# Moving three W1 pieces, their sums and four tile statistics around the first block products of a spectral and Mish network

## Chip, core and metric

The kernel runs on one core of one Trainium2 chip. Its time is device microseconds (us). The time before is the median of eight runs; a profile of one further look at the same program gives the rows quoted here. Matmuls run on TensorE (PE in the profile, its weight loads PEld), elementwise work on VectorE (DVE), ScalarE (ACT) and GpSimd (POOL). SyncE (SP) issues most of the transfers, in the order of its own queue.

## What is computed

Four layers over x of 2048 tokens by 1024 features, two kinds in turn (A, B, A, B), each added to x after a layer norm:

```
x = x + A(norm(x))     # A: rfft2, multiply by w_r + i*w_i, irfft2
x = x + B(norm(x))     # B: h = x @ w1 + b1;  act = h * tanh(softplus(h));  act @ w2
x = x + A(norm(x))
x = x + B(norm(x))
```

w1 is 1024 x 3584 and w2 is 3584 x 1024, all in bf16. The change is in layer B, which runs twice with the same weights.

## The kernel before

Every engine has its own instruction list, written out by the program in order. A helper records what each buffer was last written and read by, and puts the needed semaphore waits in front of an instruction. An engine never passes a waiting instruction, so the order in which a list is written is the order of the work.

Layer B treats the tokens as 16 tiles of 128 (index j), in four chunks of 512 (index c). The features of w1 are cut into 14 pieces of 256 columns (index fg). Normalising a tile takes these steps on VectorE: `stats_dve` (L487: two bn_stats of 512 and one aggregation), `scales` (L491: eight operations on a few numbers for a reciprocal root), and `apply` (L514, its operation on L521), which writes the normalised tile. For the first two chunks the tile is transposed on TensorE. From tile 8 on, `turned` (L1120) puts eight transposing transfers of 128 x 128 into a list, and `turn(n)` (L1131) moves n of them into SP's queue.

The chunks 0 and 1 are first multiplied plainly with pieces 0 to 5 (`mm1`, L1135). Pieces 6 to 13 are then multiplied with both chunks at once by `quads` (L1180). It sees a piece and the two chunks as 2 x 2 blocks and forms the result from seven products of four matmuls instead of eight. For that it needs sums of blocks:

- of the tokens, made by `token_sums` (L1157) on VectorE: T1, T2 and T4 by the call with `last=False`, T3 by the second call (all on L1164);
- of the weights, S1 to S4, made by `fill_slot` (L1074) on GpSimd: after the load of the piece, four operations of 128 x 512 (L1084), and a store of the piece with its sums to `w1s_scratch` (L1086). In later uses of the piece, the second layer B among them, `fill_slot` loads the stored form and GpSimd has nothing to do.

All seven products of a piece wait for all of its sums (`product`, L1184, reads `s.res` and `s.rs`). With n counting the pieces of one call of `quads`, TensorE's order in round n is A11, S2 of this piece, then A22, S4 of the one before, then S1, A12, S3 of this piece. VectorE adds the partial results (`add`, L1192, its operation on L1193). The last product of a round, S3 with T3, adds onto the bank of the second product, S2 with T2, which VectorE must first have read with its add. So the S3 of the first round waits for T3 and for that add. `after(n-1)` (L1386) is called in the middle of round n, behind S4, and puts other work there: refills of slots, loads of w2, normalisations and transposing transfers.

A slot holds one piece with its sums, 7 KB in every partition. Three slots, `early`, take pieces 6, 7 and 8. Three more, `ws`, lie where the pieces 0 to 4 of `mm1` lay, so each can be filled when `mm1` of chunk 1 is through with the pieces under it: the first after piece 1, the second after piece 3, the third after piece 4. Pieces 9, 10 and 11 go there, pieces 12 and 13 follow in the first two of them as they come free.

In the version before, the early fills name the tile buffer `xn[7].res` as something that GpSimd reads (L1356), which is how its first sums are held back behind the `apply` of tile 7. The buffer's memory is used again by the second of the token sums. Behind `mm1` come, in this order: statistics of tiles 8 to 11 and their scales, `apply` of tile 8 and its eight transposes, the fills of pieces 9 to 11, and T3 (L1373 to L1384).

Of the kernel before, what the change touches and what calls it, by code (L numbers as in the profile page):

```python
# [180 lines left out]
class KB:  # L181
# [869 lines left out]
        self.dma(self.sp, dst, self.w1.rearrange("(db dp) f -> dp db f", dp=P)[:, :, fg * 256:(fg + 1) * 256], f"w1_{writes[0].name}",  # L1051
                 reads=after, writes=writes)

    def open_slots(self, name, off, n):

        slots = []
        for i in range(n):
            b = self.alloc(f"{name}{i}", off + 7168 * i, [3584])
            b.raw = b.ap[:, 0:2048].rearrange("p (d f) -> p d f", f=256)
            b.rs = Res(f"{name}s{i}")  # L1060
            b.rs.inherit(b.res)
            slots.append(b)
        return slots
# [24 lines left out]
    def layer_B(self, li, last):  # L1088
        pe, dve, act, sp, pool = self.pe, self.dve, self.act, self.sp, self.pool
# [5 lines left out]
        def open_xt(c):  # L1095
            off = self.ob[f"XT{c}"]
            XT[c] = self.alloc(f"XT{c}", off, [8, 512])
            r_xt[c] = self.sub_res(XT[c], f"xt{c}h", 2, off, 8192)
            for r in r_xt[c]:
                r.begin()  # L1100
# [19 lines left out]
        def turned(c, t, xn):  # L1120

            x, r = XT[c], r_xt[c][t // 2]
            for db in range(8):
                def one(db=db):
                    self.dma(sp, x.ap[:, db, t * P:(t + 1) * P], xn.ap[:, db * P:(db + 1) * P], f"xt{c}_{t}", reads=[xn.res],
                             parts=[r], transpose=True)
                    if db == 7:
                        xn.unread = False
                turning.append(one)

        def turn(n):  # L1131
            for _ in range(min(n, len(turning))):
                turning.pop(0)()

        def mm1(c, fg, half=None, mid=()):  # L1135
            wb = self.w1_buf[fg]
            x = XT[c]
            tok = slice(0, 512) if half is None else slice(256 * half, 256 * half + 256)
            w = tok.stop - tok.start
            for fl in range(2):  # L1140
                if fl:
                    for f in mid:
                        f()
                ft = 2 * fg + fl
                bank = nh[0] % 3
                nh[0] += 1
                fns = []
                for db in range(8):
                    fns.append(lambda e, db=db, bank=bank, fl=fl: e.matmul(  # L1149
                        PS[:, bank, 0:w], wb.ap[:, db, fl * P:(fl + 1) * P], x.ap[:, db, tok], start=(db == 0), stop=(db == 7)))  # L1150
                self.group(fns, reads=[wb.res] + (r_xt[c] if half is None else [r_xt[c][half]]), writes=[self.r_bank[bank]])
                at, ra = AT[c % 2], r_at[c % 2][ft]
                self.op(act, lambda e, bank=bank, ft=ft: e.activation(at.ap[:, ft, tok], PS[:, bank, 0:w], ACT.Mish,  # L1153
                                                                      bias=self.B1[:, ft:ft + 1]),
                        reads=[self.r_bank[bank], self.r_b1], writes=[ra])

        def token_sums(p, last=True):  # L1157

            c0, c1 = 2 * p, 2 * p + 1
            lo, hi = [[XT[c].ap[:, 4 * k:4 * k + 4, :] for c in (c0, c1)] for k in range(2)]  # L1160
            t3 = lo[1].bitcast(F16)
            both = r_xt[c0] + r_xt[c1]
            tt = lambda dst, x, y, reads, writes: self.op(
                dve, lambda e: e.tensor_tensor(dst, x, y, ALU.subtract), reads=reads, writes=writes)  # L1164
            if last:
                tt(t3, hi[1], lo[1], r_xt[c0], r_xt[c1])
                T = self.T
                return {"B11": (lo[0], r_xt[c0]), "B21": (hi[0], r_xt[c0]), "B22": (hi[1], r_xt[c1]), "T3": (t3, r_xt[c1]),
                        "T1": (T[0].ap, [T[0].res]), "T2": (T[1].ap, [T[1].res]), "T4": (T[2].ap, [T[2].res])}
            self.T = T = [self.alloc(f"TS{i}", self.ob["TS"] + 4096 * i, [4, 512], F16) for i in range(3)]  # L1170
            tt(T[0].ap, lo[1], lo[0], both, [T[0].res])
            tt(T[1].ap, hi[1], T[0].ap, both + [T[0].res], [T[1].res])
            tt(T[2].ap, hi[0], T[1].ap, both + [T[1].res], [T[2].res])
# [6 lines left out]
        def quads(fgs, slot_of, B, after=lambda n: None):  # L1180
# [25 lines left out]
            for n in range(N + 1):  # L1206
                if n < N:
                    a, b, d, p1, u2, u3, ft = parts(n)
                    product(n, a, "A11", "B11", True)
                    self.copy(act, p1.ap, PS[:, a, :], [self.r_bank[a]], [p1.res])  # L1210
                    product(n, b, "S2", "T2", True)
                    add(u2, b, p1)
                if n:
                    _, pb, pd, q1, q2, q3, pft = parts(n - 1)
                    mish(1, pft + 1, q3.ap, q3.res)
                    product(n - 1, pb, "A22", "T4", False)
                    add(q1, pb, q1)
                    mish(0, pft + 1, q1.ap, q1.res)
                    product(n - 1, pd, "S4", "B22", False)
                    add(q2, pd, q2)  # L1220
                    mish(1, pft, q2.ap, q2.res)
                    after(n - 1)
                if n < N:
                    product(n, d, "S1", "T1", True)
                    product(n, a, "A12", "B21", False)
                    mish(0, ft, PS[:, a, :], self.r_bank[a])
                    product(n, b, "S3", "T3", False)
                    add(u3, b, p1)
                    add(u3, d, u3)
# [37 lines left out]
        W2 = [[None] * 7, [None] * 7]  # L1267

        def load_w2(h, i):
            off = (28, 32, 120, 124, 92, 96, 100)[i] * 1024 if h else self.ob["W2"] + i * 4096  # L1270
            if h and not i and W2[1][0]:
                off = 104 * 1024
            W2[h][i] = self.alloc(f"W2_{h}_{i}", off, [4, 512])
            self.dma(sp, W2[h][i].ap, w2v[:, 4 * i:4 * i + 4, h * 512:(h + 1) * 512], f"w2_{h}_{i}", writes=[W2[h][i].res])
# [6 lines left out]
        xn = {}  # L1281
# [15 lines left out]
        def residual(j):  # L1297
            self.op(dve, lambda e: e.tensor_tensor(self.XS[:, j, :], self.XS[:, j, :], YS.ap[:, j - 4, :], ALU.add),
                    reads=[YS.res], writes=[self.r_xs[j]])
# [51 lines left out]
        self.scales(6, 2)  # L1351
        for j in (6, 7):
            xn[j] = self.apply(j)
        early = self.open_slots("WE", self.ob["W2"], 3)
        for n in range(3):
            self.fill_slot(early[n], 6 + n, [xn[7].res])  # L1356
        for fg in range(2):
            mm1(1, fg, 0, mid=turns(1, 2, 3) if fg else ())
        for fg in range(2):
# [1 line left out]
        def normal(j):  # L1361
            if j % 4 == 0:
                open_xt(j // 4)
            turned(j // 4, j % 4, self.apply(j))

        for fg in range(2, 6):
            mm1(1, fg)
            if fg < 4:
                for j in range(4 * fg, 4 * fg + 4):
                    residual(j)  # L1370
            if fg == 3:
                token_sums(0, last=False)
            if fg == 4:  # L1373
                for j in range(8, 12):
                    self.stats_dve(j)
        self.xn_buf = self.xn_out + [self.alloc(f"XN{i}", self.ob["XN2"] + i * 2048, [self.D]) for i in range(2)]
        self.scales(8, 4)
        normal(8)
        turn(8)
        ws = self.open_slots("WS", self.ob["WS"], 3)  # L1380
        for n in range(3):
            self.fill_slot(ws[n], 9 + n)
        order = early + [ws[n % 3] for n in range(5)]
        B = token_sums(0)  # L1384

        def after(n):  # L1386
            if n in (3, 4):
                self.fill_slot(order[n + 3], 9 + n)
            if 2 <= n < 6:
                for i in range(2 * n - 4, min(2 * n - 2, 7)):  # L1390
                    load_w2(0, i)
            if n < 3:
                normal(9 + n)
            elif n < 7:
                self.stats_dve(9 + n)
            turn(4)
        quads(list(range(6, 14)), order, B, after)
        for i in range(7):
# [1 line left out]
        order = [ws[(n + 2) % 3] for n in range(14)]  # L1400
# [2 lines left out]
        self.xn_buf = [self.alloc(f"XN{i}", self.ob["TS"] + i * 2048, [self.D]) for i in range(4)]  # L1403
        for n in range(16):
            if n == 0:
                self.scales(12, 4)
            if n < 4:
                normal(12 + n)
            t = n % 8
            mm2(t // 4, t % 4, n // 8)  # L1410
            turn(4)
            if n == 10:
                token_sums(1, last=False)
                B = token_sums(1)
# [64 lines left out]
```

## Time and profile before

| | |
|---|---|
| median of 8 runs | 1005.75 us (1002.58 to 1008.11) |
| the profiled execution | 1005.08 us, its span 1003.3 us |
| TensorE busy | 923.3 us, 92% of the span, mean granted clock 0.983 |
| VectorE, ScalarE, GpSimd busy | 509.9, 377.4 and 157.5 us |
| first layer B: block products of pieces 6 to 13 | 173.64 to 244.84 us |
| second layer B: the same | 671.34 to 720.84 us |

All times in the rows are us from the start of the span, unless marked ns. A timeline row has its start, its length, engine, source line, operation, output and inputs, a count, and in brackets how long the engine had stood idle and what released it. A row with a count above one is a merged stretch. A row of the table by stretches has, for each engine, its busy time and its number of instructions, then the granted TensorE clock as a share of full speed.

### The profile page before, as it was taken

The page shows a single profiled execution, that of the slowest core. Times are in us where ns is not written, and L with a number is a line of the kernel's source. Part 1 is how long each engine was busy: PE and PEld are TensorE (multiplying, and loading weights), DVE is VectorE, ACT ScalarE, POOL GpSimd, SP SyncE. Part 2 cuts the span into 40 slices and gives each one's busy share as a digit, 9 for nine tenths or more (in the row PEclk, how much of TensorE's full clock was granted, in tenths as well). Part 3 has the DMA queues.
Part 4 walks back from the last instruction along what each step waited for, and adds up shares of the span by engine and source line. Part 5 has one row for each costly group of instructions (what it writes and reads, how often), then busy time and mean ns, then how long its engine had stood idle before and what let it go on. Part 6 is the DMA issues. An engine that isn't in the chain of part 4 may idle for free. (4 is left out here: it accounts for less than half of the span.)

```text
span 1003.3 us, 13599 instructions
## 1 busy us (share of the span) xinstructions
PE 923.3 (92%) x5572; PEld 489.4 (49%) x5650; DVE 509.9 (51%) x931; ACT 377.4 (38%) x531; POOL 157.5 (16%) x184
## 2 busy tenths in 40 slices
PE   0799699688999999999998997999999999999998
PEld 0667475233444444444446765754444444444443
DVE  6797468755327555524335864686611325551111
ACT  7898484243000155510007974745400015550000
POOL 4831007063500060000431200000000000000000
PEclk9999799889999999999999998999999999999999
DMA  9969732387721154230850797205761114421000
GB/s 285 278 198 323 199 98 88 88 242 226 239 61 48 43 210 152 106 110 26 206 117 20 219 227 189 111 6 179 252 215 29 45 44 162 158 95 63 32 32 21
DMA packets 140430, 136.47 MB, mean 136 GB/s; under 512 B 74368, under 2 KB 121296, under 8 KB 140368
## 3 DMA queue, kind: packets, MB, share of 16 engines
q1 hardware_dynamic: 127264, 95.26, 32.4%
q0 software_dynamic: 10928, 38.69, 11.9%
q10 hardware_dynamic: 2176, 1.66, 0.5%
q8 instruction: 44, 0.72, 0.3%
q14 instruction: 18, 0.15, 0.0%
HBM read 97.49 MB, written 33.55 MB: 131 GB/s over the span
## 5 line engine op out<-in xcount | busy, mean ns | idle before, releaser
L1239 PE MATMUL PS<-ARENA 128*128 128x512 bf16 x1756 | 385.6, 380 | 1.9
L1188 PE MATMUL PS<-ARENA 128*128 128x512 f16 (+1 forms) x1210 | 273.5, 385 | 20.7 <-DVE ARENA L1193 11.9
L1239 PEld LDWEIGHTS PS<-ARENA 128*128 128x128 bf16 x1792 | 174.9, 98 | 212.0 <-DVE ARENA L1193 0.8
L1193 DVE TENSOR_TENSOR ARENA<-PS,ARENA 128x512 f32<-128x512 f32 x220 | 152.1, 691 | 113.2 <-PE PS L1188 111.6
L1188 PEld LDWEIGHTS PS<-ARENA 128*128 128x128 bf16 x1232 | 120.8, 99 | 172.7 <-DVE ARENA L1193 15.9
L1251 DVE TENSOR_TENSOR XS<-PS,XS 128x512 bf16<-128x512 f32 x63 | 43.6, 691 | 271.1 <-PE PS L1239 271.1
L577 ACT ACTIVATE ARENA<-PS 128x512 f32<-128x512 f32 (+2 forms) x66 | 51.8, 784 | 265.1 <-PE PS L1188 254.1
L1198 ACT ACTIVATE ARENA<-ARENA,B 128x512 bf16<-128x512 f32 x132 | 95.2, 721 | 64.2 <-DVE ARENA L1193 58.2
L1084 POOL TENSOR_TENSOR ARENA<-ARENA 128x512 bf16<-128x512 bf16 x56 | 67.5, 1205 | 130.9 <-DMA ARENA<-in_B_w_dram 67.4
L1149 PE MATMUL PS<-ARENA 128*128 128x256 bf16 (+1 forms) x570 | 86.7, 308 | 0.4
L1149 PEld LDWEIGHTS PS<-ARENA 128*128 128x128 bf16 x576 | 55.4, 98 | 26.6 <-DVE ARENA L1115 0.7
L469 DVE BATCH_NORM_STATS2 BN<-XS 128x6 f32<-128x512 bf16 x99 | 64.2, 677 | 5.8 <-DMA XS<-in_A_x_dram 4.8
L1153 ACT ACTIVATE ARENA<-PS,B 128x256 bf16<-128x256 f32 (+1 forms) x72 | 38.3, 541 | 35.5 <-PE PS L1149 35.0
L1198 ACT ACTIVATE ARENA<-PS,B 128x512 bf16<-128x512 f32 x44 | 30.2, 687 | 19.4 <-PE PS L1188 19.4
L441 ACT ACTIVATE RS<-MV,EPS 128x2 f32<-128x2 f32 (+2 forms) x5 | 1.5, 298 | 95.6 <-DVE MV L472 83.7
L802 PE MATMUL PS<-ARENA 128*128 128x256 bf16 x256 | 32.4, 273 | 3.9 <-DVE ARENA L791 3.2
L780 ACT ACTIVATE ARENA<-PS 128x1024 bf16<-128x1024 f32 x32 | 33.4, 1074 | 4.5 <-PE PS L776 4.5
L728 PE MATMUL PS<-FD,ARENA 128*128 128x256 bf16 (+1 forms) x256 | 31.8, 271 | 2.4 <-DVE ARENA L646 1.3
L1023 PE MATMUL PS<-MT,ARENA 128*128 128x32 bf16 (+1 forms) x512 | 21.9, 203 | 11.2 <-DMA ARENA<-u_scratch 7.8
L784 DVE TENSOR_TENSOR ARENA<-ARENA 128x1024 bf16<-128x1024 bf16 x32 | 22.0, 687 | 19.3 <-ACT ARENA L780 13.7
L813 ACT ACTIVATE ARENA<-PS 128x1024 bf16<-128x1024 f32 x28 | 30.0, 1094 | 3.8 <-PE PS L802 3.8
L802 PEld LDWEIGHTS PS<-ARENA 128*128 128x128 bf16 x256 | 24.0, 98 | 12.0 <-DVE ARENA L791 5.7
(95 smaller groups left out, 693.2 us busy)
## 6 DMA issues: line engine op xcount, KB each, us to landing
ARENA<-in_B_w_dram SPq DMA_DIRECT2D x62, 512.0 KB, 6.4
ARENA<-w1s_scratch SPq DMA_DIRECT2D x30, 896.0 KB, 4.6
w1s_scratch<-ARENA POOLq DMA_DIRECT2D x14, 896.0 KB, 4.1
u_scratch<-ARENA SPq DMA_DIRECT2D x14, 512.0 KB, 3.5
ARENA<-u_scratch SPq DMA_DIRECT2D x14, 512.0 KB, 6.1
w_scratch<-ARENA POOLq DMA_DIRECT2D x8, 512.0 KB, 7.2
ARENA<-w_scratch POOLq DMA_DIRECT2D x8, 512.0 KB, 5.6
out_dram<-XS SPq DMA_DIRECT2D x16, 256.0 KB, 2.0
```

Of the source, the lines that this page charges most:

```text
L469: self.op(self.dve, lambda e: e.bn_stats(self.BN[:, j, 6 * h:6 * h + 6], self.XS[:, j, 512 * h:512 * h + 512]), reads=[self.r_xs[j]], part ...
L577: fn = (lambda e: e.activation(dst, src, ACT.Copy)) if scale is None else \
L780: self.op(act, lambda e: e.activation(x.ap.rearrange("p a b -> p (a b)"), ps, ACT.Copy, scale=SIG), reads=banks, writes=[x.res])
L802: fns.append(lambda e, c=c, part=part: e.matmul(ps[:, c * 256:(c + 1) * 256], yk.ap[:, part, c * P:(c + 1) * P], t[:, (128, 0)[part]:(384, ...
L1084: self.op(self.pool, lambda e, dst=A(dst), x=A(x), y=A(y), op=op: e.tensor_tensor(dst, x, y, op), reads=[b.res] + list(after), writes=[b.rs])
L1149: fns.append(lambda e, db=db, bank=bank, fl=fl: e.matmul(PS[:, bank, 0:w], wb.ap[:, db, fl * P:(fl + 1) * P], x.ap[:, db, tok], start=(db ...
L1153: self.op(act, lambda e, bank=bank, ft=ft: e.activation(at.ap[:, ft, tok], PS[:, bank, 0:w], ACT.Mish, bias=self.B1[:, ft:ft + 1]), reads= ...
L1188: self.group([lambda e, db=db: e.matmul(PS[:, bank, :], A[:, db, :], mov[:, db, :], start=(start and db == 0), stop=(db == 3), skip_group_ ...
L1193: self.op(dve, lambda e: e.tensor_tensor(dst.ap, PS[:, bank, :], x.ap, ALU.add), reads=[self.r_bank[bank], x.res], writes=[dst.res])
L1198: self.op(act, lambda e: e.activation(at.ap[:, ft, :], src, ACT.Mish, bias=self.B1[:, ft:ft + 1]), reads=[res, self.r_b1], writes=[ra])
L1239: fns.append(lambda e, i=i, ft=ft, w=W2[h][ft // 4]: e.matmul(PS[:, bank, :], at.ap[:, ft, t * P:(t + 1) * P], w.ap[:, ft % 4, :], start=( ...
L1251: self.op(dve, lambda e: e.tensor_tensor(xs, PS[:, bank, :], xs, ALU.add), reads=[self.r_bank[bank]], writes=[self.r_xs[j]])
```

## The change

The early fills now wait for a resource `gate` that stands for VectorE's instruction count behind the `apply` of tile 7; they no longer name the buffer as read. Slots of `ws` are opened and filled one by one inside the loop of `mm1`: piece 9 before `mm1` of piece 2, piece 10 before that of piece 4, piece 11 before that of piece 5. In front of the block products stand only the statistics and scales of tiles 8 and 9, and four of the transposes of tile 8. Statistics of tiles 10 and 11 go behind products 1 and 2, their scales behind product 3, and their `apply` behind products 3 and 4. Statistics of tiles 12 and 13 go behind products 5 and 6, those of 14 and 15 behind the block products. The same is written for both layers B.

```diff
-    def open_slots(self, name, off, n):
+    def open_slots(self, name, off, *ids):
         slots = []
-        for i in range(n):
+        for i in ids:
...
-        early = self.open_slots("WE", self.ob["W2"], 3)
+        gate = Res("gate")
+        gate.set_w(dve, dve.count)
+        early = self.open_slots("WE", self.ob["W2"], 0, 1, 2)
         for n in range(3):
-            self.fill_slot(early[n], 6 + n, [xn[7].res])
+            self.fill_slot(early[n], 6 + n, [gate])
...
+        ws = []
         for fg in range(2, 6):
+            if fg in (2, 4, 5):
+                ws += self.open_slots("WS", self.ob["WS"], len(ws))
+                self.fill_slot(ws[-1], 8 + len(ws))
             mm1(1, fg)
...
             if fg == 4:
-                for j in range(8, 12):
+                for j in range(8, 10):
                     self.stats_dve(j)
+        order = early + [ws[n % 3] for n in range(5)]
+        self.scales(8, 2)
         self.xn_buf = self.xn_out + [self.alloc(f"XN{i}", self.ob["XN2"] + i * 2048, [self.D]) for i in range(2)]
-        self.scales(8, 4)
         normal(8)
-        turn(8)
-        ws = self.open_slots("WS", self.ob["WS"], 3)
-        for n in range(3):
-            self.fill_slot(ws[n], 9 + n)
-        order = early + [ws[n % 3] for n in range(5)]
+        turn(4)
         B = token_sums(0)
 
         def after(n):
...
-            if n < 3:
-                normal(9 + n)
-            elif n < 7:
-                self.stats_dve(9 + n)
+            if n in (1, 2, 5, 6):
+                self.stats_dve((0, 10, 11, 0, 0, 12, 13)[n])
+            if n == 3:
+                self.scales(10, 2)
+            if n in (0, 3, 4):
+                normal((9, 0, 0, 10, 11)[n])
             turn(4)
...
             if n == 0:
+                self.stats_dve(14)
+                self.stats_dve(15)
                 self.scales(12, 4)
```

## The prediction

> **What bounds the kernel now.** I first read the table by stretches for the two runs of the same work, the block products of pieces 6 to 13 in the first and in the second layer B (columns: busy time of PE, PEld, DVE, ACT, POOL; granted clock; DMA share; GB/s).
>
> ```profile
> 173.64:244.84 71.20, 54.94 (x222) 22.96 (x225) 45.04 (x78) 26.47 (x39) 26.45 (x26) 0.88 0.61 181
> 671.34:720.84 49.50, 48.49 (x222) 21.73 (x225) 35.13 (x55) 26.67 (x39) 0.00 (x0) 1.00 0.61 189
> ```
>
> The same matmuls take 71.2 us in the first layer and 49.5 in the second, where GpSimd does nothing. So the first layer has 21.7 us that can be won, and the second next to nothing. TensorE's own timeline shows where they are.
>
> ```profile
> 173.64 3.87 PE L1188 MATMUL PS<-ARENA 128*128 128x512 bf16 x16
> 185.52 14.68 PE L1188 MATMUL PS<-ARENA 128*128 128x512 f16 x59 [8.02 <-DVE ARENA L1193]
> 203.70 21.00 PE L1188 MATMUL PS<-ARENA 128*128 128x512 bf16 x82 [3.50 <-POOL ARENA L1084]
> 228.37 13.95 PE L1188 MATMUL PS<-ARENA 128*128 128x512 bf16 x55 [3.67 <-POOL ARENA L1084]
> 243.10 1.90 PE L1188 MATMUL PS<-ARENA 128*128 128x512 f16 x8 [0.79 <-DVE ARENA L1193]
> ```
>
> Three waits: 8.0 us before the S3 product of the first round, 3.5 us for the sums of piece 9, 3.7 us for those of piece 12. The 0.8 at the end stands in the second layer too. After each of the three, weight loads start 0.43 us apart instead of 0.213: for 3.3, 5.5 and 3.4 us, which costs half of that, 1.6, 2.7 and 1.7 us. Waits and half speed make 22 us, the excess. What ends the first wait is VectorE's list, what ends the others is GpSimd's and SP's:
>
> ```profile
> 168.94 2.17 DVE L1164 TENSOR_TENSOR ARENA<-ARENA 128x2048 f16<-128x2048 bf16 x1
> 173.46 2.48 DVE L1164 TENSOR_TENSOR ARENA<-ARENA 128x2048 f16<-128x2048 bf16 x2 [2.35 <-POOL ARENA L1084]
> ...
> 183.65 1.22 DVE L1164 TENSOR_TENSOR ARENA<-ARENA 128x2048 f16<-128x2048 bf16 x1
> 184.78 0.68 DVE L1193 TENSOR_TENSOR ARENA<-PS,ARENA 128x512 f32<-128x512 f32 x1
> ```
>
> ```profile
> 167.30 6.06 POOL L1084 TENSOR_TENSOR ARENA<-ARENA 128x512 bf16<-128x512 bf16 x4
> 173.65 0.56 POOL L251 DMA_DIRECT2D w1s_scratch<-ARENA  x1 [0.30 <-POOL ARENA L1084]
> 198.81 4.83 POOL L1084 TENSOR_TENSOR ARENA<-ARENA 128x512 bf16<-128x512 bf16 x4 [24.60 <-DMA ARENA<-in_B_w_dram]
> ```
>
> ```profile
> 183.76 10.66 SPq L250 DMA_TRANSPOSE ARENA<-FD  x8
> 194.46 2.39 SPq L251 DMA_DIRECT2D ARENA<-in_B_w_dram  x3
> ```
>
> VectorE: T1, a wait for GpSimd, T2 and T4, from 175.86 to 183.7 the statistics, scales and `apply`, then T3 and the add that frees TensorE. GpSimd: 24.6 us idle for the load of piece 9. SP: that load is queued behind eight transposes, which could not start before `apply` of tile 8.
>
> **The change part by part.** I call r the time at which TensorE resumes with the first round's S3; before, r = 185.5.
>
> *The gate.* T2 no longer waits 2.35 us for GpSimd. But it now runs beside GpSimd's last sums, as T1 did: 2.17 us against 1.22 alone. T1 ends at 171.1, T2 at about 173.3; T4 waits for the end of GpSimd's last sum, itself put off to about 174.2, and ends at 175.4 instead of 175.9. Gain 0.5 us (at most 2.35, at least 0).
>
> *Two statistics fewer.* Four tiles took 175.86 to 181.5, 1.4 us each. Two less: gain 2.8 us. bn_stats doesn't suffer from GpSimd: a pair takes 1.28 us at 234.32, inside a stretch of sums, and 1.28 at 175.86 outside one. They come back behind products 1 and 2, and 5, 6 and the last, where VectorE has room: in a round of 5.97 us five adds of 0.69 take 3.5, and the same 1.5 us stood behind products 3 to 6 before at no cost in the second layer. Without that cover each would cost 1.4.
>
> *GpSimd busy where it was idle.* The three loads no longer wait behind transposes but on `mm1`: they can go out at about 160, 167 and 170 and land 6 to 7 us later. GpSimd then goes from piece 8 straight to pieces 9, 10, 11, four sums at a pitch of 1.23 us and a store of 0.9 each: ready at about 180, 186 and 192. This puts sums beside VectorE's scales, `apply` and T3, which had GpSimd idle before. No row shows a small operation of the scales beside a sum. Bounds: below, no delay, since bn_stats and the adds from PSUM (0.69 at 209.04, beside sums) have none. Above, each of the ten operations waits out most of a sum. The Trainium skill, page "SBUF — State Buffer", section "Who interferes with whom", speaks for the upper end, and so against this change: an operation with two SBUF inputs, or in a two-port mode, contends with a GpSimd operation that reads SBUF, and the loser is blocked for the whole of it. Trace: T1 lost 0.95, the residual additions went at one per 1.56 us beside sums against 0.61 in a row alone (4.89 for eight), and `apply` at 210.67 took 1.03 instead of 0.55 while the sum behind it was put off by only 0.07. So a sum holds the port for some 0.9 of its 1.23 us and leaves 0.3 free. By the rule taken as one operation per sum: 8 scales x 1.23 = 9.9, `apply` 1.4, T3 2.2, add 0.7, from 178.2 (175.4 + 2.8): r = 192.4. By the row's free 0.3 us, in which one or two operations of 0.16 fit, and with GpSimd's 0.9 us for a store in between: scales 2.7 instead of 1.6, `apply` 1.4, T3 2.1, add 0.7: r = 185.1. Without any delay: 178.2 + 1.6 + 0.55 + 1.2 + 0.7 = 182.3. I take r = 185.2, nearest to the `apply` row. So the first wait shrinks by 0.3 us only; the 3.3 us of the two parts above go into the port.
>
> *The second wait.* TensorE comes to piece 9 15 products after r, 14.7 us, at about 199.9. The sums are there at 180. Gone: 3.5 us, and with it the half speed behind it, 2.7. The page "TensorE: Matmul & The Clock Gate" (its Part 1) says that the half rate follows an idle window of about 3.4 us on a free-running grid; a wait of 3.5 would rarely hold a whole one, so by the rule 2.7 of this stays. The row has half speed for 5.5 us behind just this wait: I count 6.2.
>
> *The third wait.* The slot of piece 12 comes free with the S4 of piece 9, 26 products after r, at r + 24.1 = 209.3. Before, the same point was 215.8, and the load went out at 216.86 since SP was still at four transposes of 6.55. After, SP has eight transposes less in front of the fills and four fewer in all by then; it is through at about 207. So 1.0 us is won here. Then as before 6.6 us to GpSimd's start and 4.9 for sums: TensorE goes on at 220.9, having arrived at 218.1. The wait stays, 2.8 us.
>
> *What is late next.* Piece 13. Its load stands in SP's queue behind four transposes of tile 10, and these behind `apply` of tile 10, which now comes after product 3, with eight scales: 209.3 + 0.75 + 1.6 + 0.55 = 212.2; transposes 6.2 (four took 6.17 at 227.46), load out at 218.4, GpSimd at 223.8 (5.4, as before), ready at 228.7 = r + 43.5. Before, TensorE began piece 13 at 236.0 = r + 50.5. The distance shrinks by 7.0: 6.2 of the second wait and 0.8 net here. From piece 13 to the end nothing changes (8.8 us).
>
> *The rest at nothing.* Eight more small operations for the scales (1.6 us) sit behind product 3: 2.15 us there against 1.5 before, within the slack of 2.4 us that VectorE has (round of 5.97 less 3.5). Statistics of 14 and 15 (2.8) stand ahead of the first add of the w2 products, for which VectorE waited 3.3 us in the second layer; SP's transposes of tile 12 are behind ten loads anyway. In the second layer the fills are plain loads and TensorE doesn't wait: 0, between -0.2 and +0.5.
>
> Sum: 7.0 + 0.3 = 7.3 us, from 1005.1 of the profiled execution to 997.8, its span from 1003.3 to 996.0. The median of the runs is 0.7 above the profiled one: 1005.75 - 7.3 = 998.4.
>
> **The rivals.**
> - *The port hardly bites.* r = 182.4, another 2.8 us: 995.6. For it: adds and bn_stats don't notice GpSimd. Against it: T1 and `apply` do.
> - *The port bites hard.* More than one wait per two small operations, r = 187 to 190: 1000 to 1003, say 1001.4. For it: the rule. At r = 192.4 the whole gain is used up: 1005.6, no change.
> - *Slower.* The same port also blocks bn_stats: two tiles are six more operations of 0.87, r = 197.6, and 1005.75 - 7.0 + 12.1 = 1010.9. It decides once r is beyond 192.5. Against it: the row at 234.32.
> - *The fills don't come early*, because SP still holds them (a slot not free, a wait I don't see): the second wait stays and only part of the 3.3 us of VectorE is won, 1003.
>
> **How the numbers follow.** Forecast 998.4 has 0.53, the port that hardly bites 0.18, the port that bites hard 0.15, fills not early 0.05; no change at r near 192.4 0.04, slower 0.05. A change within 0.2% (2 us) is about what a measurement of this kernel can't tell from none. So faster 0.90 (all of the first three and nearly all of the fourth), same 0.05, slower 0.05. The range from 995.0 to 1002.5 takes in both ends of the port but the last, and 0.5 us of the second layer.
>
> **What would show it.** Right: sums (L1084) from 175 to about 191 without a long gap; the wait near 200 gone and full clock there; VectorE's scales and `apply` of tile 8 visibly slower than 1.6 and 0.55; the add that frees TensorE ending near 185; 2 to 4 us of waiting left before pieces 12 and 13; the block products in 63.9 us in the first layer, 49.5 in the second. Wrong: a first wait over 10 us, a load of piece 9 later than 165, a new wait in the second layer, or piece 13 delayed by over 3 us.

## The result, and the profile after

The changed kernel takes 1000.62 us (median of 11 runs, 998.47 to 1003.66), against 1005.48 for the version before (32 runs by now). The ratio is 0.9947, with an interval from 0.9936 to 0.9959: 5.3 us faster, 4.1 to 6.4. Forecast were 7.3. The profiled execution has a span of 998.3 us against 1003.3, its own time being 1000.21 us.

The table by stretches again, now of the changed kernel, first and second layer B:

```profile
174.25:240.46 66.21, 51.27 (x222) 22.15 (x224) 48.83 (x79) 26.47 (x39) 27.24 (x27) 0.92 0.54 173
666.58:715.89 49.31, 48.32 (x222) 21.79 (x225) 36.33 (x63) 26.79 (x39) 0.00 (x0) 1.00 0.45 137
```

The first layer's block products went from 71.2 to 66.2 us, which is the whole gain; the second layer's stayed at 49.3. TensorE's timeline of the changed kernel:

```profile
174.25 3.62 PE L1188 MATMUL PS<-ARENA 128*128 128x512 bf16 x16
188.15 33.69 PE L1188 MATMUL PS<-ARENA 128*128 128x512 f16 x141 [10.28 <-DVE ARENA L1193]
222.44 6.22 PE L1188 MATMUL PS<-ARENA 128*128 128x512 bf16 x28 [0.61 <-POOL ARENA L1084]
231.72 6.22 PE L1188 MATMUL PS<-ARENA 128*128 128x512 bf16 x27 [3.06 <-POOL ARENA L1084]
```

The wait before piece 9 is gone: 36 products run in one stretch (144 matmuls, of which 141 are in the trace). But the first wait has grown, from 8.02 to 10.28 us. In front of piece 12 stand 0.61 us instead of 3.67, and in front of piece 13 a new wait of 3.06. What filled the first wait is in VectorE's timeline:

```profile
178.78 0.63 DVE L499 TENSOR_SCALAR RS<-MV 128x2 f32<-128x2 f32 x1
179.44 0.17 DVE L501 TENSOR_SCALAR RS<-RS 128x2 int32<-128x2 int32 x1
179.64 0.99 DVE L510 TENSOR_TENSOR RS<-RS 128x2 f32<-128x2 f32 x1
180.67 0.16 DVE L511 TENSOR_TENSOR RS<-RS 128x2 f32<-128x2 f32 x1
180.86 0.16 DVE L512 SCALAR_TENSOR_TENSOR RS<-RS 128x2 f32<-128x2 f32 x1
181.06 1.62 DVE L510 TENSOR_TENSOR RS<-RS 128x2 f32<-128x2 f32 x1
182.72 0.16 DVE L511 TENSOR_TENSOR RS<-RS 128x2 f32<-128x2 f32 x1
182.91 1.00 DVE L512 SCALAR_TENSOR_TENSOR RS<-RS 128x2 f32<-128x2 f32 x1
183.95 1.46 DVE L521 TENSOR_SCALAR FD<-XS,MV,RS 128x1024 bf16<-128x1024 bf16 x1
185.33 2.17 DVE L1164 TENSOR_TENSOR ARENA<-ARENA 128x2048 f16<-128x2048 bf16 x1
187.41 0.68 DVE L1193 TENSOR_TENSOR ARENA<-PS,ARENA 128x512 f32<-128x512 f32 x1
```

And GpSimd in the same stretch, with no gap for a load in it any more:

```profile
175.70 4.92 POOL L1084 TENSOR_TENSOR ARENA<-ARENA 128x512 bf16<-128x512 bf16 x4
180.91 0.57 POOL L251 DMA_DIRECT2D w1s_scratch<-ARENA  x1 [0.30 <-POOL ARENA L1084]
181.50 4.92 POOL L1084 TENSOR_TENSOR ARENA<-ARENA 128x512 bf16<-128x512 bf16 x4
186.71 0.56 POOL L251 DMA_DIRECT2D w1s_scratch<-ARENA  x1 [0.30 <-POOL ARENA L1084]
187.28 4.92 POOL L1084 TENSOR_TENSOR ARENA<-ARENA 128x512 bf16<-128x512 bf16 x4
```

The eight small operations of the scales take 0.16 to 0.17 us each in the version before, and `apply` 0.55; two rows of it:

```profile
182.01 0.16 DVE L510 TENSOR_TENSOR RS<-RS 128x4 f32<-128x4 f32 x1
183.18 0.55 DVE L521 TENSOR_SCALAR FD<-XS,MV,RS 128x1024 bf16<-128x1024 bf16 x1
```

In the changed kernel four of the eight take 0.6 to 1.6: from 178.78 to 183.91 the eight last 5.1 us instead of 1.6, `apply` 1.46 instead of 0.55, T3 2.17 instead of 1.22. Together this is 5.4 us, more than the two statistics fewer (2.8) and the gate (0.6) had saved. Each operation that was held ended 0.01 to 0.03 us behind the end of a sum of GpSimd, as the one from 179.64 to 180.63 behind this:

```profile
179.46 1.16 POOL L1084 TENSOR_TENSOR ARENA<-ARENA 128x512 bf16<-128x512 bf16 x1
```

### The profile page after: what moved, and what is told of

Its sections match the earlier page's. It is cut to its first block, busy times and chain, and to the rows that moved or that the text cites. A ratio compares the mean times of both kernels' runs of the same rounds, so it can differ in the third digit from the quotient of the medians.

```text
span 998.3 us, 13614 instructions
## 1 busy us (share of the span) xinstructions
PE 919.2 (92%) x5572; PEld 488.3 (49%) x5650; DVE 520.7 (52%) x947; ACT 377.5 (38%) x531; POOL 158.3 (16%) x184
## 5 line engine op out<-in xcount | busy, mean ns | idle before, releaser
L1188 PE MATMUL PS<-ARENA 128*128 128x512 f16 (+1 forms) x1210 | 269.7, 382 | 19.5 <-DVE ARENA L1193 14.2
L1251 DVE TENSOR_TENSOR XS<-PS,XS 128x512 bf16<-128x512 f32 x63 | 43.5, 691 | 264.4 <-PE PS L1239 264.4
```

Source lines behind the costliest of these rows:

```text
L1188: self.group([lambda e, db=db: e.matmul(PS[:, bank, :], A[:, db, :], mov[:, db, :], start=(start and db == 0), stop=(db == 3), skip_group_ ...
L1251: self.op(dve, lambda e: e.tensor_tensor(xs, PS[:, bank, :], xs, ALU.add), reads=[self.r_bank[bank]], writes=[self.r_xs[j]])
```

## Experiments

The theory (of the port, by which the prediction means the access to the on-chip memory SBUF that VectorE and GpSimd share): GpSimd's sums of pieces 9 to 11, brought forward, run beside VectorE's list in front of the first S3 and slow its operations, so the early loads take back what the shorter list gives. The rival: the early loads are what gains, by removing the second wait, and VectorE's list matters little. All ratios are to the version before, on the same chip; 0.001 is 1.0 us. The edits are cut (...) to what matters. Where an edit adds lines, the profile's line numbers shift by a few.

**The gate alone.**

```diff
+        gate = Res("gate")
+        gate.set_w(dve, dve.count)
...
-            self.fill_slot(early[n], 6 + n, [xn[7].res])
+            self.fill_slot(early[n], 6 + n, [gate])
```

> The version before with the gate alone. Theory of the port: T2 no longer waits 2.35 us, but runs beside the last sum, so the add that frees TensorE comes 0.5 us earlier; the rest follows it: 0.5 us faster than before (0 to 1). Rival, a wait removed is a wait won: 2.3 us faster.

Measured: 0.9997 (0.9986 to 1.0008), so 0.3 us faster, which can't be told from nothing; a gain of 2.3 us in the total is excluded. VectorE's row shows why the removed wait isn't won. The three token sums of this kernel run with no idle time, but each beside a sum:

```profile
169.22 6.35 DVE L1164 TENSOR_TENSOR ARENA<-ARENA 128x2048 f16<-128x2048 bf16 x3
```

That is 6.35 us for three, and before it was 2.17, a wait of 2.35 and 2.48. From the start of the block products to the freeing add it is 10.5 us instead of 11.1. So 0.6 of the 2.35 us are won there. The total doesn't show even these: in this trace the load of piece 12 took 7.5 us to GpSimd's start instead of 6.6, TensorE waited 5.57 us for that piece instead of 3.67, and the block products took 72.2 us against 71.2.

**The early loads alone**, with four statistics and eight transposes in front as before.

```diff
+            if fg in (2, 4, 5):
+                ws += self.open_slots("WS", self.ob["WS"], len(ws))
+                self.fill_slot(ws[-1], 8 + len(ws))
             mm1(1, fg)
...
-        ws = self.open_slots("WS", self.ob["WS"], 3)
-        for n in range(3):
-            self.fill_slot(ws[n], 9 + n)
```

> The version before with the three loads moved ahead alone; four statistics and eight transposes in front, buffer named as read, as before. Theory of the port: GpSimd sums from 174 to 192 lie beside T4, scales (5 us instead of 1.6), apply and T3, so TensorE resumes near 191.5 instead of 185.5; the second wait is gone (6.2) and about 1 us more at pieces 12 and 13: 1 us faster than before (-2.5 to +0.5). Rival, the gain comes from the early loads and VectorE's list adds little: 5 us faster, as the whole change.

Measured: 0.9995 (0.9983 to 1.0007), 0.5 us. TensorE's timeline has no wait before piece 9, and pays for it in the first:

```profile
190.48 32.56 PE L1188 MATMUL PS<-ARENA 128*128 128x512 f16 x144 [14.76 <-DVE ARENA L1193]
225.45 6.22 PE L1188 MATMUL PS<-ARENA 128*128 128x512 bf16 x28 [2.41 <-POOL ARENA L1084]
233.79 7.90 PE L1188 MATMUL PS<-ARENA 128*128 128x512 bf16 x28 [2.12 <-POOL ARENA L1084]
```

14.76 us against 8.02. The rival's 5 us are not there.

**The statistics alone**: the change without the gate, and with the loads put back behind tile 8.

```diff
-            if fg in (2, 4, 5):
-                ws += self.open_slots("WS", self.ob["WS"], len(ws))
-                self.fill_slot(ws[-1], 8 + len(ws))
...
         normal(8)
         turn(4)
+        ws = self.open_slots("WS", self.ob["WS"], 0, 1, 2)
+        for n in range(3):
+            self.fill_slot(ws[n], 9 + n)
```

> The changed version with the three loads put back behind tile 8, there behind four transposes instead of eight, and the buffer named as read as before: statistics alone. Theory of the port: GpSimd is idle beside scales, apply and T3, TensorE resumes near 182.8; loads go out near 186, sums of piece 9 are ready near 195.5 when TensorE comes at 197.5, so no second wait either: 9.5 us faster than before, 4 us faster than the whole change. Rival, early loads are what removes the second wait: that wait stays at 3 us with its half speed, only 3 us faster than before.

Measured: 0.9926 (0.9913 to 0.9940), 7.4 us faster than before and about 2 faster than the whole change, though the two intervals touch. The first wait falls and there is none before piece 9, although its load went out only at 187.93:

```profile
184.32 33.03 PE L1188 MATMUL PS<-ARENA 128*128 128x512 f16 x144 [5.22 <-DVE ARENA L1193]
221.35 14.03 PE L1188 MATMUL PS<-ARENA 128*128 128x512 bf16 x56 [4.00 <-POOL ARENA L1084]
```

So the second wait did not need the early loads: here it went with four transposes fewer in front of those loads in SP's queue and an `apply` of tile 8 three microseconds earlier. Less came out than the 9.5 expected, since piece 12 waited 4.0 us, for a load that took 6.3 us to GpSimd's start.

**Loads early, sums held back behind T3.**

```diff
...
-                self.fill_slot(ws[-1], 8 + len(ws))
+                self.fill_slot(ws[-1], 8 + len(ws), sums=False)
...
         B = token_sums(0)
+        gate = Res("gate")
+        gate.set_w(dve, dve.count)
+        for n in range(3):
+            self.fill_slot(ws[n], 9 + n, [gate], load=False)
```

> The changed version, loads early, but GpSimd's sums of pieces 9 to 11 held back behind T3. Theory of the port: scales 1.6, apply 0.55, T3 1.2 as without a neighbour, TensorE resumes 5 us earlier than in the changed version, and pieces 9 to 11 are ready at about 187, 193 and 198, needed at 197, 203 and 209: 5 us faster than the changed version, 10 faster than before. Rival, VectorE's list is slow for another reason (its waits between small operations): as the changed version.

Measured: 0.9907 (0.9892 to 0.9923), 9.4 us faster than before, 4 faster than the change. In VectorE's timeline the same operations have their old lengths:

```profile
179.75 0.16 DVE L510 TENSOR_TENSOR RS<-RS 128x2 f32<-128x2 f32 x1
180.34 0.55 DVE L521 TENSOR_SCALAR FD<-XS,MV,RS 128x1024 bf16<-128x1024 bf16 x1
180.80 1.22 DVE L1169 TENSOR_TENSOR ARENA<-ARENA 128x2048 f16<-128x2048 bf16 x1
```

```profile
182.67 32.88 PE L1193 MATMUL PS<-ARENA 128*128 128x512 f16 x144 [4.84 <-DVE ARENA L1198]
```

The first wait is 4.84 us here. Only the time of GpSimd's sums differs from the changed kernel, so the slow operations were theirs.

**The scales twice**, for tiles 8 and 9, with the same values.

```diff
         self.scales(8, 2)
+        self.scales(8, 2)
```

> The changed version with the eight operations of the scales of tiles 8 and 9 done twice in the second and the first layer (same values). Theory of the port: beside the sums of piece 10 and 11 the second eight cost about what the first did, 3 to 5 us, and TensorE resumes that much later: 4 us slower than the changed version. Rival, the operations were slow for a reason of the first ones alone: 1.6 us slower, their own length.

Measured: 0.9995 (0.9986 to 1.0004), which is 4.8 us slower than the changed kernel; the trace has the first wait 4.5 us longer:

```profile
192.93 33.09 PE L1188 MATMUL PS<-ARENA 128*128 128x512 f16 x141 [14.79 <-DVE ARENA L1193]
```

The second eight last from 184.22 to 188.88, 4.7 us. The price of eight such operations beside sums was about 5 us in both places.

**The load of piece 13 ahead of the transposes of tile 10.** The last of the early loads of w2 goes out a product earlier too, so that it stays ahead of them.

```diff
-                for i in range(2 * n - 4, min(2 * n - 2, 7)):
+                for i in ((0, 1), (2, 3), (4, 5, 6), ())[n - 2]:
...
-            turn(4)
+            turn((4, 4, 4, 0, 8, 4, 4, 4)[n])
```

> The changed version with no transposes behind product 3 and eight behind product 4, there behind the load of piece 13 (and the last early load of w2). If that load waits only for SP's transposes of tile 10, it goes out 2.8 us earlier and the wait of 3.1 us before piece 13 falls to about 0.3: 2.7 us faster than the changed version, 8 faster than before. Rival, the slot itself comes free late or the load is slow for want of bandwidth: same as the changed version.

Measured: 0.9902 (0.9888 to 0.9917), 9.9 us faster than before, 4.5 faster than the change. In the trace the block products take 63.4 us against 66.2, the 2.8 expected; the rest of the difference lies outside them and within the spread of both. The wait before piece 13 is gone:

```profile
223.48 12.26 PE L1188 MATMUL PS<-ARENA 128*128 128x512 bf16 x55 [0.98 <-POOL ARENA L1084]
```

So the new wait before piece 13 was SP's queue, not the slot or bandwidth.

**T3 first.** T3 doesn't need any normalisation. Here it stands directly behind T4. Statistics of tiles 8 to 11 go between the products, those of 12 to 15 among the w2 products, each of which then has six transposes behind it instead of four.

```diff
-            if fg == 4:
-                for j in range(8, 10):
-                    self.stats_dve(j)
...
-        self.scales(8, 2)
...
-        normal(8)
-        turn(4)
...
-            if n in (1, 2, 5, 6):
-                self.stats_dve((0, 10, 11, 0, 0, 12, 13)[n])
-            if n == 3:
-                self.scales(10, 2)
-            if n in (0, 3, 4):
-                normal((9, 0, 0, 10, 11)[n])
+            if n in (0, 1, 4, 5):
+                self.stats_dve((8, 9, 0, 0, 10, 11)[n])
+            if n in (2, 6):
+                self.scales((8, 10)[n // 6], 2)
+            if n in (2, 3, 6, 7):
+                normal((0, 0, 8, 9, 0, 0, 10, 11)[n])
...
```

> The changed version with nothing of the normalisations in front of T3: T3 and the freeing add directly behind T4, statistics of tiles 8 to 11 behind products 0, 1, 4, 5, their scales behind 2 and 6, their apply behind 2, 3, 6, 7; statistics of 12 to 15 among the w2 products, six transposes in each of these. T3 beside one sum ends near 178, TensorE resumes near 178.7 with 1 us of waiting and full clock; 0.6 us of waiting before piece 12, 2 before piece 13: block products in 53 us, 13 us faster than the changed version, 18 faster than before. Rival, the transposes of tiles 8 to 15 now come too late for the token sums of the second half: a wait near the end of the first w2 products in both layers, and 5 us or more of it lost in each.

Measured: 0.9828 (0.9812 to 0.9845), 17.3 us faster than before. The first wait is 0.8 us; block products in 55.3 us instead of the 53 expected. Expected were 0.6 us of waiting before piece 12 and 2 before piece 13; it is the other way round, with 3.1 before piece 12 and none before piece 13:

```profile
176.55 31.25 PE L1188 MATMUL PS<-ARENA 128*128 128x512 f16 x141 [0.80 <-DVE ARENA L1193]
210.90 13.95 PE L1188 MATMUL PS<-ARENA 128*128 128x512 bf16 x55 [3.10 <-POOL ARENA L1084]
```

**T3 first and piece 13 first together.** The early loads of w2 are moved as above.

```diff
-            turn(4)
+            turn((4, 4, 4, 0, 8, 4, 4, 4)[n])
```

> The version before this one with the load of piece 13 ahead of the transposes as well: the 2 us before piece 13 fall to 0.3: 20 us faster than before. Rival as there; and if the load of piece 13 is bound by its slot, no further gain.

Measured: 0.9853 (0.9835 to 0.9871): 14.8 us faster, less than T3 first alone, though the two intervals overlap. There was nothing to win before piece 13, for which T3 first alone didn't wait. The rival named for T3 first came true here, by a few microseconds. The transposes are late for the token sums of the second half; VectorE stands for them with the adds of the w2 products behind it, and TensorE runs out of banks, all in the first layer:

```profile
315.55 4.71 PE L1239 MATMUL PS<-ARENA 128*128 128x512 bf16 x21 [3.02 <-DVE XS L1251]
```

T3 first alone was spared only just: VectorE stood 7.2 us for the same transposes there, and TensorE didn't notice.

**T3 first, SP clear ahead of pieces 12 and 13, later token sums.** The early loads of w2 are moved as above.

```diff
-            turn(4)
+            turn((0, 0, 0, 0, 8, 4, 4, 4)[n])
...
-            if n == 10:
+            if n == 13:
                 token_sums(1, last=False)
```

> The version with T3 first, with SP kept clear ahead of the loads of pieces 12 and 13 (no transposes behind products 0 to 3, eight behind product 4), and the token sums of the second half three w2 products later, behind the eleventh to the fourteenth. The load of piece 12 goes out 0.7 us earlier, the wait before it falls from 3.1 to about 2.4 us, and VectorE no longer stands 3 us for late transposes as in the run with both: 0.7 us faster than T3 first alone, 18 faster than before. Rival, the transposes come too late all the same: slower than T3 first alone, as in the run with both.

Measured: 0.9797 (0.9779 to 0.9815), median 984.97 us: 20.4 us faster than before and the best of all. Block products take 51.3 us, near the second layer's 49.3:

```profile
179.90 31.25 PE L1188 MATMUL PS<-ARENA 128*128 128x512 f16 x141 [0.82 <-DVE ARENA L1193]
211.92 12.26 PE L1188 MATMUL PS<-ARENA 128*128 128x512 bf16 x55 [0.77 <-POOL ARENA L1084]
```

Piece 12 waits 0.77 us instead of 3.10, more of a step than the 0.7 expected: counted from the end of the first wait its load goes out 1.85 us earlier and takes 4.5 us instead of 5.0. The half speed behind it is gone (12.26 against 13.95 for the same 14 products).

**The store of piece 11 later**, in the kernel with the statistics alone.

```diff
...
-            self.fill_slot(ws[n], 9 + n)
+            self.fill_slot(ws[n], 9 + n, store=n < 2)
...
                 self.fill_slot(order[n + 3], 9 + n)
+                if n == 3:
+                    self.store_slot(ws[2], 11)
```

> The run with the statistics alone, with GpSimd's store of piece 11 issued behind the sums of piece 12 instead of in front of them. Where a store of 0.9 MB went out just ahead of the load of piece 12 (before, the gate alone, the statistics alone) that load took 6.3 to 7.5 us to GpSimd's start; where it had gone out 8 us or more earlier, 4.3 to 4.6. If the store is the reason, the load takes 4.5 us here and the wait before piece 12 falls from 4.0 to about 2.2; the total falls by less, since piece 13 is next. If the transposes or the loads of w2 are the reason, it stays at 6.3.

Measured: 0.9893 (0.9876 to 0.9909). The load of piece 12 took 5.3 us to GpSimd's start, against 6.3 with the store in front; the wait before piece 12 is 3.05 us instead of 4.00, but the 14 products behind it took 15.1 us instead of 14.0:

```profile
218.07 15.11 PE L1194 MATMUL PS<-ARENA 128*128 128x512 bf16 x55 [3.05 <-POOL ARENA L1089]
```

So the store accounts for one microsecond of the slow load, in one trace of each. The rest, down to the 4.3 to 5.0 us of the kernels with early loads, stays open: other transfers differ too. (The expectation has 4.3 to 4.6 for them; with T3 first alone it was 5.0.) The total fell by 3.3 us, but the block products took 63.5 us here and 62.7 with the statistics alone, so the gain isn't theirs and isn't explained. The total of a single trace is no guide here: the block products begin at 172.17 us in this one and at 175.23 with the statistics alone, and between 172.14 and 175.46 in the three kernels with T3 first, though nothing in front of them differs within either group.

## Why the prediction held, and where it was off

The measured 1000.62 us lie in the range from 995.0 to 1002.5 because the range took in the rival that the port bites hard; the central forecast was 2.2 us too good. Two of the four signs of being wrong that the prediction names came true, if only just: the first wait is 10.28 us (over 10), and piece 13, its delay read as TensorE's wait for it, is late by 3.06 (over 3). The first wait was to shrink by 0.3 us and grew by 2.3.

- *The gate, at 0.5 us*: right. T4 ended 1.6 us after the start of the block products, 1.8 forecast; alone it gives 0.6 us in the trace.
- *Two statistics fewer, 2.8 us, bn_stats untouched by GpSimd*: right. The two tiles' statistics took 2.9 us beside sums.
- *GpSimd busy where it was idle*: the mechanism was right and one size in it was the error. Forecast were scales 2.7, `apply` 1.4, T3 2.1; measured 5.1, 1.46, 2.17. On the scale of the version before (the changed kernel's block products begin 0.6 later) r is 187.5, not 185.2. The step that failed is the 2.7 us for the scales. They leave room for one wait of 1.1 us; the other operations were to pass in the 0.3 us that a sum leaves free, "in which one or two operations of 0.16 fit", and in the 0.9 us that GpSimd spends on a store. Neither was free to that extent. Between two sums lie about 0.08 us (a sum takes 1.16 of the pitch of 1.23), and one operation passed there; two passed where a sum was over and the store not yet issued; and the stretch of the store held the longest operation, 1.62 us. So four of the eight waited, for 0.5, 0.8, 1.5 and 0.8 us, 3.6 in all instead of 1.1. The rule of the Trainium skill, page "SBUF — State Buffer", section "Who interferes with whom", that the loser is blocked for the whole of the other's operation, agrees with waits that end with a sum; taken as one operation per sum it gave r = 192.4, which was too much, as one or two more passed behind each of the first three that waited. The 2.4 us of the scales are about all by which the forecast was too good.
- *The second wait, 6.2 us*: gone, as forecast, and the half speed behind it too, which the rule of the Trainium skill, as the prediction applied it, would have left: the row was the better guide. That the early loads do it was not shown by that: the statistics alone remove it too. The prediction counted both parts as gains; taken singly the early loads give 0.5 us, which can't be told from nothing, and the statistics 7.4, and the whole change 5.3. The change does better without the early loads and the gate, or with the sums behind T3.
- *The third wait of 2.8 us, and what is late next*: the place was wrong and the sum right. The load of piece 12 took 4.3 us, not the 6.6 of the version before, so 0.6 stayed there, and piece 13, named as the next to be late, waited 3.1. From r to piece 13 it was 43.6 us; forecast were 43.5. That is close by some luck: the slot of piece 12 came free 1.0 us later than forecast, counted from r, and the load of piece 13 was 0.5 us quicker. That SP's transposes of tile 10 set it was shown by moving them.
- *The clock*: the 36 products behind r took 33.7 us, 3.0 more than at full speed, where half speed behind the first wait and small gaps had been put at 2.2; behind the 3.06 us before piece 13 there was no half speed.
- *The second layer at nothing*: right, 49.3 against 49.5 us.
- *The rivals*: that the port bites hard is what happened, with r = 187.5 (it has 187 to 190) and 1000.62 us (1000 to 1003). It had 0.15, and the forecast with r = 185.2 had 0.53.
- *A sum in the working*: the three waits and their half speeds add to 21.2 us, not 22, of an excess of 21.7. Nothing rests on it.

## What to carry to other kernels

Work that is brought forward on one engine lands beside somebody else's: ask which operations it will share a port with, above all many small ones on the path, before counting its own wait as won. First take off the waiting engine's list what the waiting product doesn't need; here that was every normalisation in front of T3, and it was worth 17 us where the change's own order gave 5. And after each wait that goes, look at the queue that must deliver the next piece.

## What the runs showed of the hardware

- A VectorE operation on two or four numbers per partition costs 0.16 us alone, and 0.6 to 1.6 where it meets a GpSimd sum of 128 x 512 (two bf16 inputs in SBUF). In the changed kernel, the one with early loads alone and the one with the scales twice, three or four of each eight were hit. bn_stats (1.27 us for a pair beside sums, 1.28 alone), and adds with one operand in PSUM, the memory that TensorE writes to (0.68 us), were not.
- The longest, 1.62 us, began each time while GpSimd was issuing a store (180.91 for 0.57 us in the rows above), and ran until the first sum behind it was over. The same at 184.64 with the early loads alone, and at 187.08 with the scales twice. So the issuing of a store seems to hold VectorE as a sum does; it was not tried by itself. Adds from PSUM and bn_stats that began in such a stretch kept their 0.69 and 0.68 us.
- A wait of TensorE of about 3 us sometimes costs only itself and sometimes more: nothing behind 3.06 in the changed kernel (granted clock 1.00 there), 1.7 us behind 3.10 with T3 first (0.50 from 211.44 to 214.86), about 3 behind 3.05 with the store later (0.50 from 217.05 to 223.87). In every trace the granted clock changes in steps of 3.41 us. Laid on the steps of its own trace, the wait of 3.10 has 2.9 us in one step, that of 3.05 has 2.03, and half speed comes in the next step; that of 3.06 falls on two steps, with 1.99 and 1.07 us, and nothing comes. In the first layer's block products, over all twelve traces, full speed turns into half speed near 2.0 us of idle time in one step; in front of the second layer B, with other matmuls, 1.8 was enough. The Trainium skill, page "TensorE: Matmul & The Clock Gate", Part 1, has a window of 3.4 us that runs free of the kernel, which the steps agree with; but it asks for at least one idle window, and here some 2.0 of the 3.4 us were enough. A wait of 2.12 us, with the early loads alone, cost 1.7 us more.
